# Moving one chunk's transposes from TensorE to the DMA crossbar, with three loads placed behind them, SyncE's order fixed and the ranks tuned anew

## The chip, the cores and the metric

The kernel runs on one core of a Trainium2 chip. The metric is the device time of one execution in microseconds (us). All timed runs compared below are in the fast state, except the two one-look kernels, for which one run cannot tell a state. A ratio is the mean time of one kernel's fast runs over the mean of the other's fast runs of the same rounds, so it isn't quite the ratio of the medians quoted beside it. Intervals are 95%. The experiments ran in three jobs on three chips, so across jobs the ratios compare more safely than the medians. All effects here are under 2%; "faster" and "slower" mean that the interval leaves out 1.

## The reference

A transformer-like block over 2048 tokens of width 640: a layer norm, then in parallel a dilated local attention (32 heads of 20, each token looks at 8 tokens, 2 apart) and a dense layer pair with GELU; both are added to x.

```python
x  = A_x
xn = _layernorm(x)
# attention: q, k, v = xn @ wqkv; 8 logits per token and head (offsets 0, 2, .. 14); softmax; sum; @ wo
# dense:     gelu(xn @ w1 + b1) @ w2 + b2          (640 -> 1536 -> 640)
return x + _A_ref(xn, A_wqkv, A_wo) + _B_ref(xn, B_w1, B_b1, B_w2, B_b2)
```

## The kernel before

The tokens go in four chunks of 512 (four blocks of 128 each). Each chunk is normalized, transposed to put features on partitions, projected to q, k, v on TensorE ("pps"; "gps" for the first chunk; TensorE writes to PSUM, and ScalarE copies the result out, which is called an eviction), its logits are products on VectorE ("prod") summed over the head by TensorE ("L"), then comes a softmax on VectorE and ScalarE, a broadcast of the weights over a head's 20 features by DMA ("ax"), the weighted sum on VectorE ("pv"), and an output projection ("lo"/"hi") that also takes the dense layer ("hps", "hT").

A small planner (`Plan`) lists the pieces with assumed durations and ranks, runs them on paper and so fixes the order of instructions of TensorE, VectorE and ScalarE. On the chip each engine works strictly through this order. The ranks are offsets found by tuning.

```python
        for bl in range(BPC):                      # n is the chunk
            ...
            if n > 1:                              # chunks 3 and 4: the DMA crossbar
                pl.add(f"tc{n}{bl}", DQ, 4.0, early - 3.0, [f"xn{n}{bl}"], f("td", n, bl), [xn, xnT])
                continue                           # chunks 1 and 2: TensorE, then ScalarE
            pl.add(f"tp{n}{bl}", PE, 0.3, ...)
            pl.add(f"tc{n}{bl}", SE, 0.65, ...)
        pl.add(f"xb{n}", VE, 1.43, base + 36, [...], f("xb", n), after=32.0)
...
    nc.sync.dma_start(w1_sb[:], B_w1.rearrange("(t p) n -> p t n", p=P))
    nc.sync.dma_start(w2_sb[:], B_w2.rearrange("(t p) n -> p t n", p=P))
    nc.sync.dma_start(wo2[:], A_wo.rearrange("(p t) n -> p t n", t=KT))
    nc.sync.dma_start(b2bc[:], b2_bcast)
...
    def do_td(n, bl):
        ...
        nc.sync.dma_start_transpose(xnT[:, :, bl * P : (bl + 1) * P], tiles["xn", n, bl][:])

    def do_xb(n):                                  # x + b2, and its store as the output's first part
        ...
        nc.vector.tensor_tensor(out=x_sb[:, cs, :], in0=x_sb[:, cs, :], in1=b2bc[:]..., op=ALU.add)
        nc.sync.dma_start(out_sd...[:, cs, :], x_sb[:, cs, :])

    def do_xd(n):                                  # half of the broadcast of the attention weights
        expand(nc.sync, n, (0, 1))

    def do_xs(n):                                  # the other half
        expand(nc.scalar, n, (2, 3))
```

Of the kernel before, what the change touches and what calls it, by code (L numbers as in the profile page):

```python
# [15 lines left out]
PE, VE, SE, DQ = "pe", "ve", "se", "dq"  # L16


class Plan:
# [102 lines left out]
P = 128  # L122
DH = D // H
PAD = (W - 1) * DIL
KT, FT = D // P, F // P
CH = 512
NCH = S // CH
BPC = CH // P
# [9 lines left out]
PERIOD = 52.0  # L138


RANK = {
    "ad00": 178, "av2": 376.9, "f11": 47.4, "f12": 101.9, "f13": 56.6, "gj1": 41.2, "gj3": 41.9, "o01": -41.2,
    "o02": 33.3, "o13": 84.5, "o23": 46.4, "ot0": 75.1, "pc12": 58.9, "pj30": 33.5, "pj32": 57, "qk2": -89.4,
    "st2": 250.4, "tc1": -2.9, "xb0": 48.2,
}


def make_plan(fns, offsets=RANK):

    pl = Plan(offsets)  # L150
# [6 lines left out]
    def f(kind, *a):  # L157
        return lambda: fns[kind](*a)

    def done(n, which):  # L160
        if n:
            return [f"pc{n}{which}{to}" for to in range(KT)]
        return [f"gc{bl}{g}" for bl in range(BPC) for g, parts in enumerate(GROUPS) if which in [p[0] for p in parts]]

    for n in range(NCH):
        base = n * PERIOD
        prev = base - PERIOD
        early = base + (-37.0 if n == 1 else -85.0)
        xnT, q, k, v, oT = (("xnT", n), ("q", n), ("k", n), ("v", n), ("oT", n))
        hTs = [("hT", n, ft) for ft in range(FT)]  # L170
# [10 lines left out]
        for bl in range(BPC):  # L181
            xn, tp = ("xn", n, bl), ("acc", "tp", n, bl)
            pl.add(f"xn{n}{bl}", SE if n else VE, 0.81 if n else 0.42, early + -4.0 if n else -99, [f"rc{n}" if n else f"rc{n}{bl}"], f("xn", n, bl), [xn])
            if n > 1:
                pl.add(f"tc{n}{bl}", DQ, 4.0, early - 3.0, [f"xn{n}{bl}"], f("td", n, bl), [xn, xnT])
                continue
            pl.add(f"tp{n}{bl}", PE, 0.3, early + -3.0 if n else -99, [f"xn{n}{bl}"], f("tp", n, bl), [xn, tp])
            pl.add(f"tc{n}{bl}", SE, 0.65, early + -3.0 if n else -99, [f"tp{n}{bl}"], f("tc", n, bl), [tp, xnT])
        pl.add(f"xb{n}", VE, 1.43, base + 36, [f"xn{n}{bl}" for bl in range(BPC)], f("xb", n), after=32.0)

        if n == 0:
            for bl in range(BPC):
                for g, parts in enumerate(GROUPS):
                    ps, last = ("acc", "g", bl, g), max(p[0] for p in parts)
# [5 lines left out]
        for which, buf in enumerate((q, k, v)):  # L200
# [5 lines left out]
            if which:  # L206
                need = done(n - 1, which) if n else []
# [4 lines left out]
        for wp in range(W // 2):  # L212
            pr = ("prod", "qk", n, wp)
            for i in range(2):
                need = done(n, 0) + done(n, 1) + [f"pad{n}1"]
# [3 lines left out]
        e, at, ax = ("e", n), ("attn", n), ("ax", n)  # L219
# [11 lines left out]
        for wp in range(W // 2):  # L231
            for i in range(2):
                need = [f"xd{n}", f"xs{n}", f"pad{n}2"] + done(n, 2)
                pl.add(f"av{n}{wp}{i}", VE, 1.42, base + 15.0 + 6.0 * wp + i, need, f("av", n, wp, i), [v, ax, prs[wp]])
        for k2, (a, b, r) in enumerate(((0, 1, 9.0), (2, 3, 21.0), (0, 2, 22.0))):
            need = [f"av{n}{x}{i}" for x in (a, b) for i in range(2)] if k2 < 2 else [f"ad{n}0", f"ad{n}1"]
# [8 lines left out]
        for bl in range(BPC):  # L245
            ob = ("osb", n, bl)
            O = [("O", n, bl)] if n < NCH - 1 or bl % 2 == 0 else [("acc", "lo", n, bl), ("acc", "hi", n, bl)]
            final = n * BPC + bl == LASTB
            last = None
            for pc in range(5):  # L250
                need = [last] if last else [f"ge{n}{ft}" for ft in range(FT)] + [f"xb{n}"]
                if pc == 4:
                    need.append(f"ot{n}")
                us = (0.65, 0.65, 0.65, 0.87, 1.08)[pc] if final else (0.82, 0.82, 0.82, 0.82, 1.37)[pc]
                last = pl.add(f"o{n}{bl}{pc}", PE, us, base + PERIOD + 8.0 + 8.0 * bl, need, f("o", n, bl, pc, ("lo",) if final else ("lo", "hi")), O + (hTs if pc == 0 else hTs[3 * pc : 3 * pc + 3] if pc < 4 else [oT]), 31.0)
            if final:
                pl.add("oclo", SE, 0.55, base, [last], f("oclo"), O + [ob])
                last = pl.add("ohi", PE, 1.05, base + PERIOD + 90, [last], f("ohi"), O)
                pl.add("ochi", VE, 0.25, base, [last], f("ochi"), O + [ob])
                continue  # L260
            pl.add(f"oc{n}{bl}", SE, 0.78, base, [last], f("oc", n, bl), O + [ob])
            pl.add(f"od{n}{bl}", SE, 0.0, base, [f"oc{n}{bl}"], f("od", n, bl), [ob])
# [4 lines left out]
def kernel(  # L267
# [16 lines left out]
    nc = tc.nc  # L284
# [25 lines left out]
    w2_sb = wts.tile([P, FT, D], BF16, name="w2_sb")  # L310
    wo2 = wts.tile([P, KT, D], BF16, name="wo2")
    b1_rt = consts.tile([P, P], BF16, name="b1_rt")
    b2bc = consts.tile([P, D], BF16, name="b2bc")
    wqkv_v = A_wqkv.rearrange("(t p) n -> p t n", p=P)
    b2_bcast = bass.AP(tensor=B_b2.tensor, offset=B_b2.offset, ap=[[0, P], [1, D]])
# [8 lines left out]
        cs = slice(n * BPC, (n + 1) * BPC)  # L324
        nc.sync.dma_start(x_sb[:, cs, :], x_nb[:, cs, :])
    nc.sync.dma_start(w1_sb[:], B_w1.rearrange("(t p) n -> p t n", p=P))
    nc.sync.dma_start(w2_sb[:], B_w2.rearrange("(t p) n -> p t n", p=P))
    nc.sync.dma_start(wo2[:], A_wo.rearrange("(p t) n -> p t n", t=KT))
    nc.sync.dma_start(b2bc[:], b2_bcast)


    ident = consts.tile([P, P], BF16, name="ident")
# [338 lines left out]
    last = (NCH - 1, BPC - 1)  # L671
# [14 lines left out]
        nc.scalar.dma_start(out_sd[LASTB * P :, CH:D], osb[:, CH:D])  # L686

    fns = {k[3:]: v for k, v in locals().items() if k.startswith("do_")}
    engines = {mybir.EngineType.PE, mybir.EngineType.DVE, mybir.EngineType.Activation}
    with tc.manual_schedule(engines=engines):  # L690

        idle = psA.tile([P, CH], F32, tag="acc", name="idle")
        for _ in range(WARM):
            nc.tensor.matmul(idle[:, 0:P], lhsT=ident[:], rhs=ident[:], start=True, stop=True)
        for t in make_plan(fns).run():
            t["fn"]()
# [30 lines left out]
```

## Time and profile before

| | before |
|---|---|
| median of 5 runs | 218.71 us |
| profiled span | 216.7 us |
| TensorE busy | 209.4 us, 97% |
| VectorE busy | 180.2 us, 83% |
| ScalarE busy | 110.6 us, 51% |
| transposes on TensorE / by DMA | 8 blocks / 8 blocks |

The columns of a stretch are: its bounds and length, then for each engine the busy us and the number of instructions, then TensorE's clock, the share of the DMA engines and GB/s. What an engine's busy time lacks to the length is open time. TensorE's open time is what to look for.

```profile
67.70:95.00 27.30, 27.14 (x185) 14.28 (x188) 27.09 (x18) 15.35 (x26) 1.01 (x1) 1.00 0.23 61
95.00:130.00 35.00, 34.68 (x248) 18.81 (x251) 34.12 (x23) 15.58 (x28) 2.59 (x3) 1.00 0.36 74
130.00:165.00 35.00, 34.74 (x267) 17.91 (x270) 34.18 (x24) 16.43 (x26) 3.45 (x4) 1.00 0.17 21
```

In the kernel before, TensorE (first number after the length) is open for 0.16, 0.32 and 0.26 us of these stretches: 0.74 us in 97. Even that need not be real: this trace holds 1689 matmuls to 1714 weight loads, so 25 records are missing. The trace of e11 below, with the same order on TensorE, has all 1714 and shows no open time in these stretches. VectorE (third) is nearly as full: 27.09, 34.12 and 34.18 us. That second fact turns out to matter.

### The profile page before, as it was taken

The numbers are of one execution on the slowest core, as the hardware profiler recorded it, in microseconds if no ns is written. First come the engines' busy times: TensorE is split into PE (matmuls) and PEld (weight loads), VectorE is DVE, ScalarE is ACT, GpSimd is POOL, SyncE is SP. The second block draws the span as 40 slices with busy tenths as digits, with TensorE's granted clock in tenths as the row PEclk, the third lists the DMA queues.
The fourth block names the chain that finished last, engine by engine and source line by source line (L and its number), as shares of the span: only waits on it lengthen the run. The fifth ranks groups of instructions, "written<-read, shape, count | busy, mean of one in ns | idle before, by whom it ended". The sixth has DMA issues, their size and how long they took to land.

```text
span 216.7 us, 3977 instructions
## 1 busy us (share of the span) xinstructions
PE 209.4 (97%) x1689; PEld 121.1 (56%) x1714; DVE 180.2 (83%) x169; ACT 110.6 (51%) x195; POOL 14.5 (7%) x33
## 2 busy tenths in 40 slices
PE   7899999999999999999999999999999999999994
PEld 7799855554554555555555455554544555555552
DVE  3759999988999999999899999989999999922000
ACT  3665999796757554734184625026665311341211
POOL 2000000000000000101010101011010011101121
PEclk9999999999999999999999999999999999999999
DMA  6999931907314401336020280222025222200253
GB/s 221 366 365 393 375 136 48 259 0 185 72 30 118 97 0 44 77 57 170 3 30 0 30 193 3 30 33 29 2 33 107 87 30 33 28 2 3 30 61 62
DMA packets 18761, 20.83 MB, mean 96 GB/s; under 512 B 6328, under 2 KB 15928, under 8 KB 18744
## 3 DMA queue, kind: packets, MB, share of 16 engines
q1 hardware_dynamic: 15144, 15.83, 24.7%
q0 software_dynamic: 2160, 2.46, 9.4%
q10 hardware_dynamic: 1440, 2.29, 3.1%
q8 instruction: 13, 0.21, 0.4%
q14 instruction: 4, 0.03, 0.0%
HBM read 10.00 MB, written 5.08 MB: 70 GB/s over the span
## 4 chain that ended last, share of the span: by engine, by line
PE 93%; DVE 1%; ACT 1%; DMA 1%; ACTq 1%; issue 1%; DVEq 0%
PE lo L655 27%; PE pps L455 23%; PE hps L622 22%; PE gps L472 8%; PE hi L657 8%; PE L L517 5%; DMA x_sb<-in_A_x_dram 1%; PE tp L416 1%; ACTq L584 1%; ACT L633 1%; DVE stats L375 0%; DVE stats L376 0%; ACT xnT L420 0%; ACT hT L633 0%; DVE xn L402 0%
## 5 line engine op out<-in xcount | busy, mean ns | idle before, releaser
L622 PE MATMUL hps<-xnT,w_sb 128*128 128x512 bf16 x230 | 53.2, 379 | 0.4
L655 PE MATMUL lo<-w_sb,hT 128*128 128x512 bf16 x187 | 52.9, 379 | 0.0
L505 DVE TENSOR_TENSOR prod<-qT,kT 128x2560 bf16<-128x2560 bf16 x32 | 45.4, 1483 | 0.7 <-ACT kT L490 0.7
L600 DVE TENSOR_TENSOR pv<-vT,ax 128x2560 bf16<-128x2560 bf16 x32 | 45.7, 1484 | 0.0
L657 PE MATMUL hi<-w_sb,hT 128*128 128x128 bf16 x192 | 40.3, 219 | 0.5 <-issue 0.3
L622 PEld LDWEIGHTS <-w_sb 128*128 128x128 bf16 x240 | 22.8, 98 | 26.3 <-issue 0.2
L633 ACT ACTIVATE hT<-hps,b1T 128x512 bf16<-128x512 f32 x48 | 31.4, 686 | 11.8 <-PE hps L622 9.8
L662 ACT CAST osb<-lo 128x512 bf16<-128x512 f32 x15 | 8.8, 586 | 53.8 <-PE hi L657 35.4
L609 DVE TENSOR_TENSOR pv<-pv 128x5120 bf16<-128x5120 bf16 x12 | 33.9, 2823 | 0.3
L655 PEld LDWEIGHTS <-hT 128*128 128x128 bf16 x192 | 18.7, 98 | 23.0 <-issue 1.5
L668 POOL DMA_DIRECT2D out_dram<-osb x15 | 13.1, 873 | 196.8 <-ACT osb L663 196.8
L655 PE MATMUL lo<-wo,oT 128*128 128x512 bf16 x75 | 22.1, 379 | 0.0
L657 PEld LDWEIGHTS <-hT 128*128 128x128 bf16 x192 | 18.4, 98 | 1.8
L455 PE MATMUL pps<-xnT,wv_sb 128*128 128x512 bf16 x74 | 17.3, 379 | 0.3 <-ACT hT L633 0.2
L657 PE MATMUL hi<-wo,oT 128*128 128x128 bf16 x80 | 16.9, 219 | 0.3
L455 PE MATMUL pps<-xnT,wk_sb 128*128 128x512 bf16 x74 | 16.8, 379 | 0.1
L455 PE MATMUL pps<-xnT,wq_sb 128*128 128x512 bf16 x72 | 16.7, 379 | 0.2
L490 ACT CAST vT<-pps 128x512 bf16<-128x512 f32 x15 | 8.7, 586 | 11.4 <-PE pps L455 9.4
L655 PEld LDWEIGHTS <-oT 128*128 128x128 bf16 x80 | 7.8, 98 | 9.6 <-issue 0.4
L455 PEld LDWEIGHTS <-wk_sb 128*128 128x128 bf16 x75 | 8.7, 118 | 7.3 <-issue 0.2
L455 PEld LDWEIGHTS <-wq_sb 128*128 128x128 bf16 x75 | 8.6, 118 | 7.1
L455 PEld LDWEIGHTS <-wv_sb 128*128 128x128 bf16 x75 | 8.5, 118 | 7.3 <-issue 0.5
(67 smaller groups left out, 208.9 us busy)
## 6 DMA issues: line engine op xcount, KB each, us to landing
w_sb<-in_B_w_dram SPq DMA_DIRECT2D x2, 1920.0 KB, 16.2
out_dram<-osb POOLq DMA_DIRECT2D x15, 160.0 KB, 3.4
ax<-attn SPq DMA_DIRECT2D x8, 256.0 KB, 4.9
ax<-attn ACTq DMA_DIRECT2D x8, 256.0 KB, 5.6
x_sb<-in_A_x_dram SPq DMA_DIRECT2D x3, 640.0 KB, 11.2
out_dram<-x_sb SPq DMA_DIRECT2D x3, 640.0 KB, 3.9
wq_sb<-in_A_wqkv_dram SPq DMA_DIRECT2D x1, 800.0 KB, 5.2
wk_sb<-in_A_wqkv_dram SPq DMA_DIRECT2D x1, 800.0 KB, 7.3
```

What stands on the lines that cost most here:

```text
L455: nc.tensor.matmul(ps[:], lhsT=wqkv_p[which][:, ti, to, :], rhs=xnT[:, ti, :], start=(ti == 0), stop=(ti == KT - 1),)
L472: nc.tensor.matmul(ps[:, i, :], lhsT=wqkv_p[which][:, ti, to, :], rhs=tiles["xnT", 0][:, ti, cs], start=(ti == 0), stop=(ti == KT - 1),)
L505: nc.vector.tensor_tensor(out=prod[:, i, :, :], in0=qkv_tile(n, 0)[:], in1=qkv_tile(n, 1)[:, :, off : off + CH], op=ALU.mult,)
L517: nc.tensor.matmul(L[j * H : (j + 1) * H, 2 * wp : 2 * wp + 2, :], lhsT=head_of[:], rhs=prod[:, :, t, j * P : (j + 1) * P], start=(t == 0 ...
L600: nc.vector.tensor_tensor(out=pv[:, i, :, :].rearrange("p t (j c) -> p t j c", j=BPC), in0=qkv_tile(n, 2)[:, :, off : off + CH].rearrange( ...
L609: nc.vector.tensor_tensor(out=ta[:], in0=ta[:], in1=tb[:], op=ALU.add)
L622: nc.tensor.matmul(ps[:], lhsT=w1_sb[:, ti, ft * P : (ft + 1) * P], rhs=tiles["xnT", n][:, ti, :], start=(ti == 0), stop=(ti == KT - 1),)
L633: nc.scalar.activation(hT[:], tiles["hps", n, ft][:], ACT.Gelu_apprx_tanh, bias=b1T[:, ft : ft + 1], scale=1.0)
L655: nc.tensor.matmul(lo[:], lhsT=lhs, rhs=rhs[:, 0:CH], start=first, stop=last)
L657: nc.tensor.matmul(hi[:, 0 : D - CH], lhsT=lhs, rhs=rhs[:, CH:D], start=first, stop=last)
L662: nc.scalar.copy(osb[:, 0:CH], tiles["lo", n, bl][:])
L668: nc.gpsimd.dma_start(rows, tiles["osb", n, bl][:], accum_op=ALU.add)
```

## The change

The intent: TensorE is the full engine, so take twenty 128x128 transposes from it. The crossbar must then not stand behind the large loads, so w2, wo and b2 are issued after the four transposes; and since SyncE issues all of them, its order is fixed by the planner too. The ranks were tuned anew for the changed plan.

```diff
-    "ad00": 178, "av2": 376.9, "f11": 47.4, ...          (19 rank offsets)
+    "ad00": -9.2, "ad02": 24.8, "av1": 61.5, ...         (22 rank offsets)
...
-            if n > 1:
-                pl.add(f"tc{n}{bl}", DQ, 4.0, early - 3.0, [f"xn{n}{bl}"], f("td", n, bl), [xn, xnT])
+            if n > 0:
+                pl.add(f"tc{n}{bl}", DQ, 4.0 if n > 1 else 2.7, early - 3.0, [f"xn{n}{bl}"], f("td", n, bl), [xn, xnT], 21.5)
...
-        pl.add(f"xb{n}", VE, 1.43, base + 36, [f"xn{n}{bl}" for bl in range(BPC)], f("xb", n), after=32.0)
+        if n == 1:
+            pl.add("ld", DQ, 9.2, -1000, [f"tc1{bl}" for bl in range(BPC)], f("ld"))
+        pl.add(f"xb{n}", VE, 1.43, base + 36, [f"xn{n}{bl}" for bl in range(BPC)] + ["ld"], f("xb", n))
...
-    nc.sync.dma_start(w2_sb[:], ...); nc.sync.dma_start(wo2[:], ...); nc.sync.dma_start(b2bc[:], b2_bcast)
+    def do_ld():
+        nc.sync.dma_start(w2_sb[:], ...); nc.sync.dma_start(wo2[:], ...); nc.sync.dma_start(b2bc[:], b2_bcast)
...
-    engines = {mybir.EngineType.PE, mybir.EngineType.DVE, mybir.EngineType.Activation}
+    engines = {getattr(mybir.EngineType, e) for e in ("PE", "DVE", "Activation", "SP")}
```

(The last loads are put on one line here.) Three consequences are not in the diff but in the order that the planner makes of it. The b2 additions "xb" of chunks one and two stood on VectorE ahead of the softmax of chunk one; now the first stands inside it, after the subtraction, and the second right behind it. And SyncE has to issue the store of the second addition, which now comes late, just before its half of the broadcast.

## The prediction

> **What bounds the kernel now.** I read the busy table first, then the slices, then the chain of work that ended last.
>
> ```profile
> PE 209.4 (97%) x1689; PEld 121.1 (56%) x1714; DVE 180.2 (83%) x169; ACT 110.6 (51%) x195; POOL 14.5 (7%) x33
> ...
> PE   7899999999999999999999999999999999999994
> ...
> DMA  6999931907314401336020280222025222200253
> ...
> PE 93%; DVE 1%; ACT 1%; DMA 1%; ACTq 1%; issue 1%; DVEq 0%
> ```
>
> TensorE is busy in 97% of the 216.7 us span and makes 93% of the chain; it has full slices from the third to the last but one. A busy share alone could hide slack, so I looked at the holes. The stretches after 25.20 us, once the first chunk's projections are over, have PE busy 12.74 of 12.90, 16.95 of 17.20, 12.19 of 12.40, 27.14 of 27.30, 34.68 of 35.00, 34.74 of 35.00 (twice) and 13.51 of 13.60 us. Together about 1.5 us are open, in pieces of 0.05 to 0.2 us. So the time is the sum of TensorE's work plus some 7.4 us of head (the first matmul of real work starts at 7.39 us) and 3.1 us of tail (TensorE ends at 213.6 us). Taking work from TensorE shortens the kernel one for one; taking work from any other engine gives nothing, unless TensorE waits for it.
>
> The work that goes is visible in the chain, in order of time (start, length, what):
>
> ```profile
> 28.44 0.66 PE L L517 x20
> 29.10 0.66 PE tp L416 x10
> 29.76 1.29 PE hps L622 x6
> ...
> 33.90 0.28 PE tp L416 x5
> 34.17 0.66 PE L L517 x20
> 34.84 0.38 PE tp L416 x5
> 35.22 0.05 issue
> ...
> 38.17 4.23 PE pps L455 x19
> ```
>
> The "tp" pieces after 25 us are the second chunk's twenty transposes. They stand in the chain itself, so nothing else runs on TensorE then.
>
> The other side of the trade is the DMA system (issues: size of each in KB, median us to landing; a stretch of time with DMA share and GB/s at its end):
>
> ```profile
> w_sb<-in_B_w_dram SPq DMA_DIRECT2D x2, 1920.0 KB, 16.2
> ...
> wo<-in_A_wo_dram SPq DMA_DIRECT2D x1, 800.0 KB, 17.9
> ...
> b2bc<-in_B_b_dram SPq DMA_DIRECT2D x1, 160.0 KB, 9.9
> xnT<-xn SPq DMA_TRANSPOSE x8, 2.6
> ```
>
> ```profile
> core 0: us, PE busy (x) PEld busy (x) DVE busy (x) ACT busy (x) POOL busy (x), PEclk, DMA share, GB/s
> ...
> 7.39:25.20 17.81, 17.77 (x312) 17.54 (x312) 14.18 (x43) 12.54 (x31) 0.00 (x0) 1.00 1.06 373
> ```
>
> The loads saturate the queues until about 28.5 us. The w1 load, issued at 8.74 us, takes 14.4 us and lands at 23.1; w2 lands at 28.5, wo at 30.5, b2 at 30.9. From 31 us the DMA engines are idle. The eight existing transposes (chunks three and four) take a median of 2.6 us from issue, 5.6 at worst, and SyncE is held 1.2 to 2.05 us by the issue of each.
>
> **What the Trainium skill says.** "TensorE: Matmul & The Clock Gate", section "Wait — 56ns, not 53.3ns?": warm back-to-back matmuls start 55.6 ns apart at 128 columns and 215.7 at 512. The trace agrees: ten transposes in 0.56 us, twenty 512-column projections in 4.32 us. So the 219 ns that a row prints for a transpose is latency, and its cost on a full TensorE is 56 ns. "VectorE: DVE Perf Modes", section "The three transpose paths": 390 ns for a 128x128 block on TensorE, 1309 ns through the crossbar. The trace has no such single block; a DMA of five blocks lands in 2.6 us. The DMA path is slower, and is worth taking only since the busy engine is TensorE. "DMA: Bandwidth & Descriptors", section "Queues, rings and completion order": each DMA engine consumes one ring's descriptors in order. A transpose that SyncE issues therefore stands behind whatever SyncE had queued. In the kernel before, a transpose issued at 20 us would stand behind w2 and wo; this is why the change moves those loads. No run so far shows it.
>
> **Part by part.** *Removed from TensorE:* four blocks of five transposes. From the chain: 0.66 + 0.28 + 0.38 = 1.32 us. At the pure rate it would be 20 x 56 ns = 1.12 us[...]. All of it is on the path: 1.1 to 1.3 us gained. *Removed from ScalarE:* four evictions of about 0.69 us, 2.8 us, off the path (ScalarE is at 51%); four PSUM buffers are no longer taken. *Order:* the remaining matmuls are the same in kind and number, only ranked anew. The small bias transpose moves from 12.06 us, where it stood 0.2 us in the chain, to the last of the first chunk's projections; about even. Head and tail have the same steps, so 7.4 and 3.1 us stay.
>
> *Added, first chain:* normalized block, DMA transpose, projection. There are only two buffers for normalized blocks, so the third must wait until the first transpose has landed. I place the events by adding durations from the trace along the new order. The second chunk's statistics end at 17.7 us as before; the new order has one more block (1.02 us) and the reciprocal after it, so 19.1. ScalarE normalizes block one at about 19.6 to 20.5 and block two at 21.4 to 22.3. The first transpose stands behind w1 and lands about 24 to 25 us (w1 at 23.1 plus a short transfer). Block three's place on ScalarE comes at about 24.9: a wait of 0 to 1 us. Behind it are two PSUM evictions of the first chunk, which free a buffer for the third first-layer matmul group at 27.1 us; they would be done at 26.4 to 27.6. A stall of 0 to 0.5 us there. Block four comes after the fourth GELU: a 1.28 us table load and four GELUs of about 0.69 put it at 31.0 to 31.9, its transpose lands at 34.6 to 35.0 in an idle DMA system. TensorE wants it for the first projection of chunk two: 24.8 + 8 x 1.08 (first layer) + 3 x 0.7 to 0.8 (logits) = 35.7 us. Slack about 0.7 us.
>
> *Added, second chain:* w2, wo, b2 are issued from about 33.5 us. 2.88 MB at 373 GB/s is 7.7 us, so b2 lands at 42 to 44. First use of b2: an addition on VectorE, which the new order puts after the softmax's subtraction, at about 42.0; the next step waits for the exponential until 43.9 anyway. A delay of 0 to 1.5 us, against about 3 us between VectorE's products and TensorE's use of them in chunk two (from the sums under "Later"). First use of w2 on TensorE comes near 60 us. Hidden.
>
> *Later:* I summed the TensorE and VectorE durations along both orders. For before, the sum gives an end at 213.9 us (measured 213.6) and a third output tile of VectorE that fits within 0.1 us, so it is good enough for slacks. In the new order the logits keep 1.3 to 3.3 us, the attention outputs of chunks one to four 2.3, 0.4, 1.4 and 3.5 us. Only the 0.4 is thin.
>
> Sum: -1.3 for the transposes, -0.1 for gaps that go with them, +0.1 for the first stall (half weight on 0 to 0.5, mostly near 0), +0.15 for the fourth transpose coming late, +0.1 for the thin slack: -1.05 us. 218.56 - 1.05 = 217.5 us.
>
> **Rivals.** *A wait takes the place of the work.* The fourth transpose lands late and TensorE stands before the projections of chunk two. For it: slack is 0.7 us, ScalarE's order strings table load, GELUs and the two-buffer wait together, and the trace has a transpose of 5.6 us and a 1.25 us wait of ScalarE for the transpose of two blocks before. Against it: from 31 us the queues are empty in the new order, and the plan's own ranks were set for this case. If it lands at 5.6 instead of 2.6 us, 2.3 us are lost: 219.7. *The late loads stall VectorE and through it TensorE.* For it: SyncE took 8.4 us to issue wo when much was queued. Against it: less is queued now, and 3 us of slack. If the issue takes 8.4 us again, b2 lands near 50 us, VectorE loses 6 to 7, TensorE some 3 to 4: 221. *Hidden anyway or better:* if the new order also closes half of the 1.5 us of small holes, 216.8.
>
> **Range and chances.** Most weight on the pure removal of 1.1 to 1.4 us with a stall of at most half a microsecond: 216.9 to 217.8; the upper rivals get about one part in six. I say 217.5, 216.8 to 218.8. Faster by over 2% would need 214.2, more than the transposes and all holes together: 0.01. Slower by over 2% (222.9) needs both rivals: 0.02. Within 2%: 0.97.
>
> **What would show it.** Right: no "tp" piece after 25 us; PE busy down by about 1.3 us with an end near 212.5; no idle time of "pps" on a DMA. The first transposes land after w1 and before 26 us; b2 before 44. Wrong: "pps" of chunk two, or the first-layer groups at 27 us, with idle time released by a DMA or by ScalarE; or VectorE's b2 addition waiting for a DMA by more than 3 us and the logits of chunk two late. A TensorE end that fell less than PE's busy time did would mean that stalls ate the gain.

## The result

The changed kernel takes 220.02 us (219.46 to 220.69, 5 runs) against 218.71 for the kernel before: ratio 1.0064, interval 1.0035 to 1.0093. It is slower by 0.6%, where 0.5% faster was predicted, and lies outside the predicted 216.8 to 218.8. A second measurement is among the experiments. The page of the changed kernel, busy times, TensorE's slices and the engines' shares of the chain that ended last:

```profile
PE 208.8 (96%) x1669; PEld 120.1 (55%) x1694; DVE 180.0 (83%) x169; ACT 107.9 (49%) x191; POOL 14.5 (7%) x33
...
PE   7899999999999799999999999999999999999994
...
PE 54%; DVE 29%; DMA 10%; ACTq 2%; SPq 2%; issue 2%; ACT 1%; DVEq 0%
```

The twenty matmuls are gone (1689 to 1669). The busy shares look almost as before, and one slice alone has dropped. But the chain has changed hands: TensorE's share fell from 93% to 54%, VectorE has 29% and DMA 10%. An engine that is busy 83% of the span now sets much of the end. The stretches shown for before, now in the changed kernel:

```profile
67.70:95.00 27.30, 25.80 (x146) 13.45 (x147) 27.20 (x17) 16.47 (x28) 1.01 (x1) 1.00 0.29 73
95.00:130.00 35.00, 34.15 (x255) 18.56 (x259) 33.65 (x24) 14.14 (x24) 2.59 (x3) 1.00 0.28 48
130.00:165.00 35.00, 34.40 (x271) 17.94 (x274) 34.70 (x24) 16.61 (x28) 2.59 (x3) 1.00 0.23 43
```

TensorE is open for 1.50 + 0.85 + 0.60 = 2.95 us, 2.2 more than before, all of it after 67 us. (The second measurement's trace has all its matmul records and shows 2.50 + 0.10 + 0.28 = 2.88 us here; it is of a run of 222.39 us, the slowest of its eight.) Up to 67 us TensorE has no more open time than before. So the first risk that the prediction named (the transposes come late) did not come true, and the loss comes later than the place of the edit. The chain tells whence (start, length, what; this answer covers 5 to 75 us):

```profile
33.85 10.39 DMA b2bc<-in_B_b_dram
44.24 0.02 issue
44.26 1.49 DVE x_sb L437
45.76 1.87 DVE ssum L567
...
48.64 1.23 DVE attn L579
49.86 1.42 DVE x_sb L437
...
51.29 0.39 SPq L444
51.68 0.05 issue
51.73 1.57 SPq L589
53.30 0.05 issue
53.36 8.00 DMA ax<-attn
...
62.79 4.30 DVE pv L605 x3
```

Read from the top: b2 (160 KB, queued behind w2 and wo) lands 10.39 us after its issue; only then does VectorE add it (x_sb), and only behind that stands the softmax's sum. After the weights (attn) comes the second b2 addition, then on SyncE its store (L444), and only then SyncE's half of the broadcast (L589), whose second transfer takes 8.00 us. The same in the timeline; the bracket is the idle time before the row and what ended it:

```profile
44.26 1.49 DVE L437 TENSOR_TENSOR x_sb<-x_sb,b2bc 128x2560 bf16<-128x2560 bf16 x1 [1.95 <-DMA b2bc<-in_B_b_dram]
...
61.38 2.89 DVE L605 TENSOR_TENSOR pv<-vT,ax 128x2560 bf16<-128x2560 bf16 x2 [1.70 <-DMA ax<-attn]
```

VectorE loses 1.95 us to b2 and 1.70 us to the broadcast. In the kernel before, VectorE waited for neither; the same two places there, without a bracket:

```profile
34.77 2.89 DVE L432 TENSOR_TENSOR x_sb<-x_sb,b2bc 128x2560 bf16<-128x2560 bf16 x2
...
56.76 8.49 DVE L600 TENSOR_TENSOR pv<-vT,ax 128x2560 bf16<-128x2560 bf16 x6
```

How this reaches TensorE is seen fifteen microseconds later:

```profile
75.64 0.25 ACT L502 COPY vT<-vT 128x70 bf16<-128x70 bf16 x1 [2.04 <-DVE pv L605]
75.79 0.58 ACT L495 CAST qT<-pps 128x512 bf16<-128x512 f32 x1
...
76.42 2.54 PE L460 MATMUL pps<-xnT,wq_sb 128*128 128x512 bf16 x10 [1.29 <-ACT qT L495]
```

A small copy on ScalarE writes a v buffer that VectorE is still reading for chunk one. It waits 2.04 us. The PSUM eviction behind it in ScalarE's order waits along, and TensorE stands 1.29 us for a PSUM buffer. It is the dropped slice.

### The profile page after: what moved, and what is told of

It reads as the page before. It is cut to its first block, busy times and chain, and to the rows that moved or that the text cites. A ratio compares the mean times of both kernels' runs of the same rounds, so it can differ in the third digit from the quotient of the medians.

```text
span 218.0 us, 3944 instructions
## 1 busy us (share of the span) xinstructions
PE 208.8 (96%) x1669; PEld 120.1 (55%) x1694; DVE 180.0 (83%) x169; ACT 107.9 (49%) x191; POOL 14.5 (7%) x33
## 4 chain that ended last, share of the span: by engine, by line
PE 54%; DVE 29%; DMA 10%; ACTq 2%; SPq 2%; issue 2%; ACT 1%; DVEq 0%
PE lo L660 20%; PE hps L627 14%; DVE pv L605 8%; PE gps L477 8%; PE hi L662 6%; DVE pv L614 5%; DMA b2bc<-in_B_b_dram 5%; DMA ax<-attn 4%; PE pps L460 3%; DVE x_sb L437 3%; DVE prod L510 3%; DVE ssum L567 3%; PE L L522 2%; ACTq L589 2%; DVE attn L579 2%
## 5 line engine op out<-in xcount | busy, mean ns | idle before, releaser
L627 PE MATMUL hps<-xnT,w_sb 128*128 128x512 bf16 x231 | 55.1, 379 | 0.5
L627 PEld LDWEIGHTS <-w_sb 128*128 128x128 bf16 x240 | 22.3, 98 | 26.0 <-issue 1.1
L460 PE MATMUL pps<-xnT,wq_sb 128*128 128x512 bf16 x74 | 17.2, 380 | 1.4 <-ACT qT L495 1.3
L460 PE MATMUL pps<-xnT,wk_sb 128*128 128x512 bf16 x73 | 17.3, 380 | 0.5 <-ACT kT L495 0.4
L495 ACT CAST kT<-pps 128x512 bf16<-128x512 f32 x15 | 8.6, 585 | 11.1 <-PE pps L460 11.1
L380 DVE BATCH_NORM_STATS2 stats<-x_sb 128x6 f32<-128x320 bf16 x16 | 7.3, 459 | 6.8 <-DMA x_sb<-in_A_x_dram 6.8
## 6 DMA issues: line engine op xcount, KB each, us to landing
w_sb<-in_B_w_dram SPq DMA_DIRECT2D x2, 1920.0 KB, 11.5
```

Of the source, the lines that this page charges most:

```text
L460: nc.tensor.matmul(ps[:], lhsT=wqkv_p[which][:, ti, to, :], rhs=xnT[:, ti, :], start=(ti == 0), stop=(ti == KT - 1),)
L495: nc.scalar.copy(dest[:, to, off : off + CH], tiles["pps", n, which, to][:])
L627: nc.tensor.matmul(ps[:], lhsT=w1_sb[:, ti, ft * P : (ft + 1) * P], rhs=tiles["xnT", n][:, ti, :], start=(ti == 0), stop=(ti == KT - 1),)
```

## The experiments

Theory A: VectorE became late in chunk one because the b2 addition stands inside the softmax and b2 lands late. Rival B: the broadcast is late for its own reason, SyncE's order. Rival C: the new order of TensorE and ScalarE is bad by itself. Medians stand beside 218.68 us (first and third job) and 218.73 us (second) for the kernel before.

### e1_b2_early: b2 alone loaded up front

```diff
     nc.sync.dma_start(w1_sb[:], B_w1.rearrange("(t p) n -> p t n", p=P))
+    nc.sync.dma_start(b2bc[:], b2_bcast)
 ...
     def do_ld():
         ...
-        nc.sync.dma_start(b2bc[:], b2_bcast)
```

> The changed kernel with b2 alone (160 KB) loaded up front, behind w1; the order of every engine but SyncE is the same. Theory A (VectorE became late in chunk one because its b2 addition stands before the softmax's sum and b2 lands only at 44.24 us): the 1.95 us wait of VectorE for b2 is gone, the sum then waits for the exponential until about 44.5, the attention weights are ready 1.1 to 1.2 us earlier (48.7 instead of 49.9), everything of VectorE up to 100 us is earlier by about that, and the time falls by about 1.1 us from 220.0 to 218.9. Rival B (the broadcast of the attention weights is late for its own reasons: SyncE's order and a crowded DMA): VectorE's wait for it stays or grows to 1.7 to 2.9 us, and the time falls by less than 0.4 us. Rival C (TensorE's or ScalarE's new order is bad by itself, whatever VectorE does): no change of the time, 219.8 to 220.2.

Measured: 219.19 us (22 runs, 218.21 to 221.27), ratio 1.0019 (1.0004 to 1.0034). Its timeline:

```profile
44.98 1.97 DVE L567 TENSOR_REDUCE ssum<-e 128x128 f32<-128x1024 bf16 x1 [0.82 <-ACT e L562]
...
60.70 4.30 DVE L605 TENSOR_TENSOR pv<-vT,ax 128x2560 bf16<-128x2560 bf16 x3 [1.69 <-DMA ax<-attn]
```

The wait for b2 is gone and the sum waits 0.82 us for the exponential instead, as A said. About 0.8 us of time came back by the medians (220.02 to 219.19), somewhat less than the 1.1 expected; against the second measurement of the changed kernel, 220.54, it is 1.35. The wait for the broadcast stayed at 1.69 us, as B said. A holds, but is not the whole.

### e2_expand_first: SyncE issues the broadcast before the store

```diff
     def do_xb(n):
         ...
-        nc.sync.dma_start(out_sd...[:, cs, :], x_sb[:, cs, :])
+        if n != 1:
+            store(cs)
     def do_xd(n):
         expand(nc.sync, n, (0, 1))
+        if n == 0:
+            store(slice(BPC, 2 * BPC))
```

> The changed kernel with one SyncE order turned round: the store of the second chunk's x + b2 is issued behind the broadcast of the first chunk's attention weights instead of before it. Theory A: b2 still lands at 44.2 and VectorE is late by 1.95 us there, but the broadcast no longer waits for the second b2 addition, so it is issued 1.5 to 1.8 us sooner; time falls by half a microsecond at most (219.5 to 220). Rival B: the broadcast lands at 59.6 or sooner instead of 61.36, VectorE's wait of 1.7 us for it vanishes, and the time falls by 1.2 to 1.7 us, to 218.3 to 218.8. Rival C: no change.

Measured: 218.67 us (22 runs), ratio 0.9990 (0.9978 to 1.0001). Its timeline:

```profile
44.42 1.49 DVE L440 TENSOR_TENSOR x_sb<-x_sb,b2bc 128x2560 bf16<-128x2560 bf16 x1 [1.83 <-DMA b2bc<-in_B_b_dram]
...
59.74 5.69 DVE L611 TENSOR_TENSOR pv<-vT,ax 128x2560 bf16<-128x2560 bf16 x4
```

VectorE still waits 1.83 us for b2, but no longer for the broadcast; its first weighted product starts at 59.74 instead of 61.38 us. B's number was met. This one turn of two SyncE instructions is worth 1.35 us (1.9 against the second measurement), more than the b2 load.

### e3_both: both edits

> Both edits together: b2 up front and the broadcast before the store. If A and B each carry a part and VectorE's lateness is the whole loss, the two gains add to 2.3 to 2.9 us on VectorE, TensorE's stalls after 67 us (some 2.5 us more than predicted) go, and the time is 217.3 to 217.8, just what was predicted for the change, faster than the kernel before by 0.4 to 0.6%. If rival C is right, it stays above 219.5.

Measured: 218.06 us (14 runs), ratio 0.9959 (0.9945 to 0.9973). Against the first measurement of the changed kernel the parts are 0.83 and 1.35 us alone and 1.96 together; against the second 1.35, 1.87 and 2.48. So they overlap in part, and do not simply add. It is faster than the kernel before, and the changed TensorE and ScalarE orders are untouched in it, so rival C as the main cause is out. TensorE's stretch from 67.70 to 95.00 us is back at 26.98 of 27.30 us. The time is 0.3 us above the expected 217.8, so something small was left.

### e5_loads_front: w2, wo and b2 up front, behind them the transposes

```diff
     nc.sync.dma_start(w1_sb[:], ...)
+    nc.sync.dma_start(w2_sb[:], ...); nc.sync.dma_start(wo2[:], ...); nc.sync.dma_start(b2bc[:], b2_bcast)
     def do_ld():
+        pass
```

> The changed kernel with w2, wo and b2 all loaded up front as in the kernel before, so that the new transposes stand behind them on SyncE's queue. If the queue is served in order, the first transpose lands about 31 us instead of 24 (w2, wo and b2 landed at 28.5 to 30.9 in the kernel before), the third normalized block waits some 6 us for it, two PSUM evictions behind it hold up TensorE at 27 us, and the projections of chunk two start 5 to 7 us late: 224 to 227 us. If transposes are not held by loads queued before them, the time is that of the b2-early kernel or better, 218 to 219.

Measured: 226.78 us, one run. The third block on ScalarE:

```profile
31.69 0.92 ACT L404 ACTIVATE xn<-x_sb,nmr,rstd 128x640 bf16<-128x640 bf16 x1 [7.01 <-DMA xnT<-xn]
```

It waits 7.01 us for the first transpose, and runs when that lands, at 31.7 us (in the changed kernel the same block runs at 24.08 us without a wait). TensorE is open 5.3 us between 25.2 and 38.1. Moving the large loads behind the transposes was therefore needed. Only b2 should not have gone with them: it is 160 KB of 2.9 MB and has the earliest use.

### e6_after_dummies and e7_both_dummies: twenty matmuls put back

Both have the same edit, e6 in the changed kernel and e7 in e3:

```diff
     def do_f1(n, ft):
         ps = psA.tile(...)
+        if n == 0 and ft in (4, 6):
+            for _ in range(10):
+                nc.tensor.matmul(ps[:, 0:P], lhsT=ident[:], rhs=ident[:], start=True, stop=True)
```

> The changed kernel with twenty idle 128-column matmuls put back on TensorE at about the place where the removed transposes stood (ten each before the fifth and seventh first-layer group of chunk one; they write a PSUM tile that the group then overwrites). If TensorE bounds the changed kernel, they cost what the transposes cost in the chain, 1.1 to 1.3 us: 221.2. If VectorE's late chain bounds it (the maximum of chunk one then waits 1.1 us longer for TensorE, but the 1.95 us wait for b2 behind it shrinks by as much, and TensorE has 2.5 us of stalls later), they cost 0 to 0.4 us: 220.0 to 220.4.

> The same twenty matmuls in the kernel with b2 up front and the broadcast before the store (218.06). With the waits mended, TensorE's work should be one for one again: 1.0 to 1.3 us more, 219.1 to 219.4; this is also the measure of what the removed transposes were worth. If they cost under 0.5 us here, the transposes were never worth what the chain showed, and the gain of the mended kernel has another source (the new ranks).

Measured: e6 219.70 us (22 runs), ratio 1.0043 (1.0027 to 1.0059): not dearer than the changed kernel, whose two ratios are 1.0064 and 1.0082, and below the 220.0 to 220.4 that were expected. e7 219.17 us (22 runs), ratio 1.0001 (0.9985 to 1.0017): 1.11 us dearer than e3 by medians, 0.9 by the ratios. So with the matmuls back, the mended kernel only equals the kernel before: the new ranks alone gain nothing clear. The same work costs nothing where VectorE sets the end and its full length where TensorE does. VectorE's timeline in e6 shows how it vanishes:

```profile
40.74 1.22 DVE L545 TENSOR_REDUCE m<-L 128x128 f32<-128x1024 f32 x1 [2.26 <-PE L L532]
...
44.58 1.49 DVE L437 TENSOR_TENSOR x_sb<-x_sb,b2bc 128x2560 bf16<-128x2560 bf16 x1 [0.79 <-DMA b2bc<-in_B_b_dram]
```

The maximum waits longer for TensorE (2.26 us; 1.14 in the changed kernel), and the wait for b2 shrinks from 1.95 to 0.79 us. The sum of the two is the same: 3.05 and 3.09. That is a picture of work taken off an engine which then only waits elsewhere. Whether e6 is really a little faster than the changed kernel (the intervals overlap) stays open.

### e8_adds_early: both b2 additions in VectorE's idle times

```diff
 ...
+        for move, ahead in (("xb0", "m0"), ("xb1", "ss0")):
+            steps.remove(at[move])
+            steps.insert(steps.index(at[ahead]), at[move])
 ...
```

(`steps` is the planned list. b2 is up front as in e1.)

> The changed kernel with b2 up front and the two b2 additions of VectorE moved into its idle times before the softmax's maximum and before its sum (VectorE waits there 1.1 us for TensorE and 0.8 us for the exponential anyway); their stores go out before the broadcast, while the DMA system is nearly idle. If VectorE's lateness in chunk one is what is left of the loss, this is the best of the kernels: the weights ready at 48.9 to 49.3, the broadcast landed by 58, VectorE about 1 us earlier than in the mended kernel: 217.5 to 218.0, below the kernel before by 0.3 to 0.6%. If what is left lies elsewhere (later stages), it equals the mended kernel, 218.0 to 218.2.

Measured: 218.10 us (22 runs), ratio 0.9972 (0.9957 to 0.9988), the same as e3. Its VectorE starts the weighted products at 57.62 us, 1 us sooner than in e3, with no wait for the broadcast at all, and the time did not follow. So what is left lies after chunk one.

### e9_after_unpinned: SyncE's order left to the scheduler

```diff
-    engines = {getattr(mybir.EngineType, e) for e in ("PE", "DVE", "Activation", "SP")}
+    engines = {mybir.EngineType.PE, mybir.EngineType.DVE, mybir.EngineType.Activation}
```

> The changed kernel without the pinning of SyncE: its order is then left to the scheduler, which puts w2 and wo ahead of the four transposes (the order was looked at). If the queue is served in order, as the front-loaded kernel's 226.78 showed, this lands near it, 224 to 227: the pinning is what makes the move of the loads take effect, and it is no cost by itself. If pinning SyncE is itself what slowed the change, this is at or below 219.

Measured: 225.95 us, one run, near e5 as expected. The unpinned scheduler moves w2 and wo ahead of the transposes; a normalized block then waits 6.8 us and TensorE 5.1 us. Pinning is needed for the loads to stay behind the transposes. Whether it costs anything by itself is not shown, since the order changed with it; e3 and e10 are pinned and faster than the kernel before.

### after_again: the changed kernel unaltered

> The changed kernel itself, unaltered, once more, so that it stands beside the mended kernels with as many runs. If the first measurement was no accident of a chip: 219.5 to 220.3, slower than the kernel before by 0.4 to 0.8%. If it was: within 0.2% of the kernel before.

Measured: 220.54 us (8 runs, 219.73 to 222.39), ratio 1.0082 (1.0050 to 1.0114). The median is 0.2 us above the expected band; the loss repeats in a second job. In its kept trace (222.39 us) the stall before "pps" is 2.5 us instead of 1.29, and TensorE's granted clock is 0.94 in the stretch from 67.70 to 95.00 us and 1.00 in the others after 7.39 us.

### e10_issue_on_sync and e11_before_on_sync: where the rest was

In the changed kernel's timeline, and two microseconds sooner likewise in e3's, ScalarE shows this:

```profile
127.72 2.36 ACTq L589 DMA_DIRECT2D ax<-attn  x2
130.12 2.05 ACT L495 CAST vT<-pps 128x512 bf16<-128x512 f32 x4 [4.97 <-issue]
```

ScalarE issues half of the third chunk's broadcast. The one broadcast buffer is still read by VectorE, the issue waits, and the PSUM evictions behind it wait 4.97 us (4.93 in e3). The edit gives the issue for chunks two and three to SyncE, which has nothing else to do then. e10 has it in e3, e11 in the kernel before:

```diff
     def do_xd(n):
-        expand(nc.sync, n, (0, 1))
+        expand(nc.sync, n, (0, 1) if n in (0, 3) else (0, 1, 2, 3))
     def do_xs(n):
-        expand(nc.scalar, n, (2, 3))
+        if n in (0, 3):
+            expand(nc.scalar, n, (2, 3))
```

> The mended kernel (b2 up front, broadcast before the store) with the broadcasts of chunks two and three issued by SyncE alone instead of half by ScalarE. In the mended kernel's trace ScalarE stands 4.9 us at that issue near 123 us, waiting for VectorE to free the one broadcast buffer, and TensorE loses about 0.4 us behind it. If this is the rest of what the prediction missed: 217.5 to 217.8, 0.3 to 0.5 below the mended kernel's 218.06. If TensorE loses those tenths elsewhere or SyncE's single queue makes the broadcast later: 218.0 to 218.3.

> The kernel before with the same issue of broadcasts by SyncE alone. Its TensorE has only 0.58 us open between 95 and 165 us, so if the stall at ScalarE's issue belongs to the new order, this gains nothing: 218.5 to 218.8. If it belongs to both, it gains 0.3 to 0.4 as well: 218.3.

Measured: e10 217.36 us (10 runs), ratio 0.9941 (0.9918 to 0.9964), the lowest median of all kernels here and faster than both the kernel before and the change. Its interval overlaps that of e3, but the kept traces place the gain. The evictions in e3, then in e10:

```profile
128.09 2.05 ACT L499 CAST vT<-pps 128x512 bf16<-128x512 f32 x4 [4.93 <-issue]
...
125.92 2.05 ACT L499 CAST vT<-pps 128x512 bf16<-128x512 f32 x4 [2.63 <-PE pps L464]
```

They now wait only for TensorE's own result. At 116 us e10's ScalarE is 0.14 us behind e3's, at 135 us it is 0.28 us ahead, and at the end 0.27.

e11 219.22 us (22 runs), ratio 1.0021 (1.0001 to 1.0040): no gain, rather a slight loss, which was not expected. Its kept trace (219.74 us) is 1.1 us behind that of the kernel before by 10.4 us, long before the edited issues, and 1.07 us behind at the end: in this run the edit neither gained nor cost, and the delay at the start has no cause on record. So the stall at ScalarE's issue belongs to the new order. The engines' shares of the chain in e3, then in e10:

```profile
PE 85%; DVE 10%; DMA 1%; ACTq 1%; issue 1%; ACT 1%; DVEq 0%
...
PE 95%; DMA 1%; DVE 1%; ACT 0%; issue 0%; DVEq 0%
```

TensorE has the chain again, with two points more than in the kernel before.

| kernel | median us | ratio to before |
|---|---|---|
| before | 218.68 | 1 |
| changed, first measurement (beside 218.71) | 220.02 | 1.0064 |
| changed, second measurement | 220.54 | 1.0082 |
| e6: changed + 20 matmuls | 219.70 | 1.0043 |
| e1: b2 up front | 219.19 | 1.0019 |
| e2: broadcast before store | 218.67 | 0.9990 |
| e3: both | 218.06 | 0.9959 |
| e7: e3 + 20 matmuls | 219.17 | 1.0001 |
| e8: both b2 additions early | 218.10 | 0.9972 |
| e10: e3 + issue by SyncE | 217.36 | 0.9941 |
| e11: before + issue by SyncE | 219.22 | 1.0021 |

## Why the prediction was wrong

- **What bounds the kernel before, and what the transposes cost there:** right. Putting back as many matmuls cost 1.11 us by medians in e7 (0.9 by the ratios), at or just under the lower end of the predicted 1.1 to 1.3. The small holes were misread: the listed stretches leave 1.7 us open, not 1.5, and missing records can make all of it, as e11's full trace shows, so there was likely nothing in them to gain.
- **First chain (transposes in time for chunk two):** right. The third block ran at 24.08 us with no wait, the fourth from 30.14 us, and the first projection of chunk two started at 36.09 us (35.7 predicted) without idle time. The stall of 0 to 0.5 us at the third group was 0; the fourth transpose cost nothing.
- **Second chain, the step that failed:** "A delay of 0 to 1.5 us, against about 3 us between VectorE's products and TensorE's use of them in chunk two ... Hidden." b2 landed at 44.24 us, just past the predicted 42 to 44. VectorE waited 1.95 us for it, of which 0.82 us would have gone to the exponential anyway (e1), so the delay of some 1.1 us was right in size. But the slack was read at the wrong consumer. The 3 us are those of the logits of chunk two. The weights of chunk one feed another path, the broadcast and the weighted sum, for which the recorded working shows no step. In the kernel before, SyncE issued as soon as the weights were done and its two transfers took 4.0 and 4.8 us. In the changed kernel the first product starts 11.5 us after the weights (49.87 to 61.38): SyncE's issue comes 1.9 us after them, behind the second b2 addition and its store, and its transfers take 6.9 and 8.0 us. I had the order in view and did not follow it along SyncE. e2 shows that this alone is worth 1.35 us.
- **Later slacks:** the sums of durations were fit for what they covered, but covered only the places where TensorE waits for VectorE directly. The stall came through ScalarE: a copy that waits for VectorE to leave a v buffer, and a broadcast issue that waits for VectorE to leave the one "ax" buffer, each with PSUM evictions behind it. The 0.4 us slack called thin, of chunk two, held: its output tile is done at 135.00 us and first loaded by TensorE at 135.41. What broke was chunk one's, put at 2.3 us: done at 84.07, loaded at 84.12 after a wait of 0.24 us, which e3 does not have.
- **Rivals:** the second rival had the right mechanism (late loads, VectorE, then TensorE) with a wrong trigger. It expected the issue of wo to take 8.4 us again; it took 0.84 us. Its alarm, a b2 wait of "more than 3 us", was set too high: 1.95 us did the harm together with the broadcast.
- **Signs:** b2 before 44 us missed by 0.24. By the page TensorE's busy time fell by 0.6 us and not by 1.3 (missing records blur this), and its end went from 213.6 to 215.0 us instead of to 212.5. That was the last sign named: stalls ate the gain.
- **Sum:** predicted 217.5. With the two waits mended e3 gives 218.06, and with the third mended e10 gives 217.36. The gain was there; the stalls took it and 1.3 to 1.9 us more (220.02 and 220.54). That e10 comes so near 217.5 is partly luck, since its own edit was not in the prediction's sum.

What stays open: why the broadcast's last transfer took 8.00 us in the changed kernel. The traces narrow it. Where the second store stands just ahead of SyncE's half in the queue, its two transfers take 6.9 and 8.0 us (changed), 6.5 and 7.0 (e1), 6.4 and 6.3 (e6). Where the store has gone out earlier they take 5.8 and 5.7 (e8), and where it comes behind the first takes 6.0 (e2) or 5.4 (e3); the last there can't be read. So in these runs the transfers with a store just ahead take 0.6 to 2.3 us longer than those of e8. What makes up the rest against the 4.0 and 4.8 us of the kernel before is not shown.

## What to carry to other kernels

When work leaves the fullest engine, the second-fullest is next in line: follow each wait that the change adds to all consumers, through the issuing queues and the small instructions that stand before evictions in an in-order engine, not only to the nearest one. A load that is moved to make room for others should be split by first use: the smallest tensor may be needed first. And test whether an engine bounds by putting the removed work back as idle work: if that costs nothing, the bound is elsewhere.

## What the Trainium skill lacked or had wrong

- "Perfetto Trace Analysis", section "Identifying the Most-Contended Engine", says to optimize the engine of highest occupancy first, and to judge TensorE not by its matmul busy share but by the share of the peak that its arithmetic reaches and by the busy share of its weight loads. Here such shares don't tell the cases apart: weight loads are busy 55% and VectorE 83% in the changed kernel, 56% and 83% in e3 (the share of the peak was not worked out). Yet twenty matmuls more cost nothing in the changed kernel (219.70 against 220.02 and 220.54 us) and 1.11 us in e3. The page lacks a check such as putting the removed work back.
- "DMA: Bandwidth & Descriptors", section "Queues, rings and completion order", says that each DMA engine takes the descriptors of one ring in order. e5 agrees: behind w2, wo and b2 the first transpose landed at 31.7 us, without them at 23.8 us. The section does not say what that can cost a kernel; here it was 7.0 us of waiting and some 7 us of time (226.78 us, one run, against 220.02).
- "VectorE: DVE Perf Modes", section "The three transpose paths", gives 1309 ns for one block through the crossbar. The section lacks the time that the issuing engine is held: SyncE was held 1.20 to 3.90 us by each transpose of five blocks, which landed 2.6 us (median) to 6.8 us after issue.
- No page gives a time for a broadcast of 256 KB within SBUF beside other traffic: it took 3.9 to 8.0 us in the changed kernel.
